# Moving the load ring of a two-attention decode kernel to the front of SBUF, in slots of 63744 bytes

## The chip, the core and the metric

The kernel runs on one core of one Trainium2 chip. The metric is the device time of one execution in microseconds (us). Three runs of the kernel before took 1010.08, 1009.97 and 1012.16 us; the median is 1010.08 us. Beside them stands one profiled execution, in which every instruction and every DMA packet was recorded. Its span, from the first to the last instruction, is 1008.4 us.

## The reference

One token `x` (448 numbers) goes through two attention blocks with a cache of 8192 positions, and a gate mixes the results:

```python
def block(x, k_cache, v_cache, wq, wo):       # A: 16 K/V heads; B: 8, each used by two q heads
    q = (x @ wq).reshape(16, 256)
    scores = einsum("hd,hkd->hk", q, k_cache) * 256 ** -0.5     # 8192 positions
    p = softmax(scores)
    o = einsum("hk,hkd->hd", p, v_cache)
    return o.reshape(16 * 256) @ wo
g = sigmoid((x * gate_w).sum())
out = g * A(x) + (1 - g) * B(x)
```

All is float32. Every number of the caches is used once (B's K and V for two heads at a time), so 432.02 MB have to come in from HBM and 1.8 KB go out.

## The kernel before

**The stream.** The host lays all inputs out as one stream, `in_stream_dram`, in the order in which the kernel uses them. `plan()` (lines 47 to 88) cuts it into 54 *fills*. A fill is what one buffer of the ring holds: 128 rows (one for each partition) of up to 15872 float32, that is 63488 bytes a partition and 8.13 MB in all. Fills 0 to 50 are one DMA each; fill 0 carries eight numbers more a row (`XG`). The last three fills are cut into 12 smaller DMAs, so that little is left to compute when the last bytes land. Within a fill stand pieces: tiles of K (`k`), of V (`v`), and the weights `wq` and `wo` of one of eight sets of heads (`NS`).

**The ring.** Line 464 takes a buffer from the pool `ring`, which has three (`SLOTS = 3`, line 34). Line 468 issues the DMA on SyncE's queue (SP). SP waits there until every instruction that used the slot's last content has ended; no other queue moves bulk data. The text calls the three buffers the first, second and third slot; fill n is in the slot n mod 3.

**The work on a fill.** Line 471 hands each piece to its function. `project` (line 211) makes q on TensorE from `wq`. `scores` (line 244) does the K tiles of two of a set's three units on TensorE (L255), then minimum (DVE, L261), exponential (ACT, L264) and a 32x32 transpose (DVE, L267). `scores_by_row` (line 271) does the third unit's K tiles on VectorE: a product in place in the slot (L277) and a sum (L281). `attend` (line 299) multiplies V by the weights of the softmax on TensorE (L307). `combine`, `column`, `project_o` and `emit_set` fold a head into the output, in small instructions. At the end L397 adds the last heads, L482 copies the result out of PSUM and L483 stores it.

**Order.** The schedule is manual (line 111): each engine runs its instructions in the order of the text, and the loop over `LOADS` (line 463) fixes it.

**Where the tiles lie.** Pools take their place in SBUF in the order in which they are opened, and tiles are padded to 32 bytes. In front lie 4224 bytes that the program keeps (4096 of them are `dynamic_dma_scratch_size`). Then come `const` (line 104) with 4736 bytes of masks, zeros, `xz`, `qb` and the like; `ring` (line 105); and `small` (line 106), with all other scratch tiles (`px`, `pr`, `qa`, `ob` and so on). A slot is 15880 float32, 63520 bytes. So the slots begin at bytes 8960, 72480 and 136000 of each partition, which are 0, 32 and 64 past a multiple of 256, and the third ends at 199520, which is 2912 bytes past 196608 (192 x 1024).

Of the kernel before, what the change touches and what calls it, by code (L numbers as in the profile page):

```python
# [7 lines left out]
F32 = mybir.dt.float32  # L8
# [6 lines left out]
P = 128  # L15
# [12 lines left out]
FULL = 15872  # L28
# [5 lines left out]
SLOTS = 3  # L34
# [6 lines left out]


XG = 2 * (KF + 1)
ATOM = {"xg": XG, "k": 2 * DH, "v": 2 * DH, "wq": 2 * DH, "wo": D}


def plan():

    size = {"xg": XG, "k": ROWS * DH, "v": ROWS * DH, "wq": WQ, "wo": 8 * D}
    per = len(UNITS) * NT  # L50
# [15 lines left out]
    for kind, i in items[:items.index(last[0])]:  # L66
        at, left = 0, size[kind]
        while left:
            step = min(left, room) // ATOM[kind] * ATOM[kind]
            if step:  # L70
# [24 lines left out]
def kernel(  # L95
# [5 lines left out]
    nc = tc.nc  # L101
    scale = DH ** -0.5

    const = ctx.enter_context(tc.tile_pool(name="const", bufs=1))
    ring = ctx.enter_context(tc.tile_pool(name="ring", bufs=SLOTS))
    small = ctx.enter_context(tc.tile_pool(name="small", bufs=2))
    ps_sc = ctx.enter_context(tc.tile_pool(name="ps_sc", bufs=2, space=PSUM))
    ps_o = ctx.enter_context(tc.tile_pool(name="ps_o", bufs=3, space=PSUM))
# [41 lines left out]
    nc.vector.tensor_scalar(rows4, rows4, 0.0, None, op0=OP.is_equal)  # L150
    any4 = const.tile([P, 1], F32, name="any4")
    nc.vector.tensor_reduce(any4, rows4, axis=AX.X, op=OP.add)
    ones = const.tile([P, 1], F32, name="ones")
    nc.vector.memset(ones, 1.0)

    in4 = const.tile([P, 2, NG], F32, name="in4")
# [258 lines left out]
    def piece(kind, i, at, view):  # L415
        n = view.shape[-1] // ATOM[kind]
        j0 = at // ATOM[kind]
        if kind == "xg":
            inputs(view[:, :KF + 1])
            GW[0] = view[:, KF + 1:]  # L420
        elif kind == "wq":
            project(i, j0, view.rearrange("p (c n) -> p c n", c=n))
            if j0 + n < 2 * KF + 1:
                pass
            elif i == 0:
                spread(0)
                prepare(GW[0])
            else:
                wait(1, spread, i)
        elif kind == "k":  # L430
            u, t = TILES[i]
            if u in BY_ROW:
                scores_by_row(u, t, 2 * j0, view.rearrange("p (j d) -> p j d", d=DH))
            else:
                scores(u, t, j0, view.rearrange("p (c n) -> p c n", c=n))
            if j0 + n < 2 * NG:
                return
            tick()
            if t == NT - 1:
                gather(u)  # L440
                wait(1, combine, u)
                wait(2, column, u)
        elif kind == "v":
            u, t = TILES[i]
            n = view.shape[-1] // DH
            attend(u, t, at // DH, n, view.rearrange("p (j d) -> p j d", d=DH))
            if at // DH + n == ROWS:
                if t == NT - 1:
                    take(u)
                    if u != TILES[-1][0]:  # L450
                        wait(1, project_o, u)
                if i >= len(TILES) - LEAD:
                    tick()
        elif kind == "wo" and i < NS - 1:
            emit_set(i, j0, view.rearrange("p (c n) -> p c n", c=n))
            if i == NS - 2 and j0 + n == 8:
                fold()
        else:
            for j in range(n):
                LAST[divmod(j0 + j, 2)] = view[:, j * D:(j + 1) * D]  # L460

    off = 0
    for fill in LOADS:
        buf = ring.tile([P, FULL + XG], F32, name="slot")
        c = 0
        for load in fill:
            n = sum(x[3] for x in load)
            nc.sync.dma_start(buf[:, c:c + n], stream[off:off + P * n].rearrange("(p n) -> p n", p=P))
            off += P * n
            for x in load:  # L470
                piece(*x[:3], buf[:, c:c + x[3]])
                c += x[3]
# [78 lines left out]
```

## Time and profile before

| What | Value |
|---|---|
| runs | 1009.97, 1010.08, 1012.16 us; median 1010.08 us |
| span of the profiled execution | 1008.4 us |
| the median less that span | 1.7 us |
| read from HBM | 432.02 MB |
| TensorE matmul busy | 584.2 us (58%) |
| VectorE (DVE) busy | 458.2 us (45%) |
| ScalarE (ACT) busy | 92.8 us (9%) |
| mean granted TensorE clock | 0.765 of full speed |

The span is the profiled execution's own time from its first to its last instruction; no other time of that execution was recorded, and what lies around it is taken to be the 1.7 us that separate it from the median of the runs. "Busy" is the time in which at least one instruction of an engine runs. The DMA rows count packets: one packet is what one of the core's 16 DMA engines moves in one go, here one partition's row of a load. A share over 100% means that packets on one engine overlap by a little.

### The profile page before, as it was taken

What the parts mean: (1) busy time and instruction counts of PE and PEld (TensorE: products, weight loads), DVE (VectorE), ACT (ScalarE), POOL (GpSimd) and SP (SyncE); (2) the same over time, 40 slices, a digit from 0 to 9 for tenths busy, and PEclk for the clock granted to TensorE, in tenths of its full rate; (3) what the DMA queues carried; (4) which work ended last, traced back from release to release, by engine and by line L of the source; (5) the groups of instructions that cost most, each with busy time, mean ns of one, the idle gap of its engine ahead of it and who ended that gap; (6) DMA issues with size and microseconds to landing.
All of it is one profiled execution on the core that took longest, in us unless ns stands there. A gap on an engine that the chain in (4) does not pass through costs nothing.

```text
span 1008.4 us, 7568 instructions
## 1 busy us (share of the span) xinstructions
PE 584.2 (58%) x3154; PEld 171.4 (17%) x3154; DVE 458.2 (45%) x644; ACT 92.8 (9%) x307; POOL 1.9 (0%) x10
## 2 busy tenths in 40 slices
PE   0855845664655555746646576655665637536567
PEld 0211211121111111212111121111211112111112
DVE  1386213961248521576214841248521585206851
ACT  0100100010100110001100000100110100101010
POOL 0000000000000000000000000000000000000000
PEclk9877787777787787877777767776787867877878
DMA  9999999999999999999999999999999999999997
GB/s 403 442 438 418 434 436 439 418 441 431 441 436 426 424 441 438 429 426 442 431 428 441 431 429 434 436 434 431 432 431 441 439 423 424 439 443 431 418 426 310
DMA packets 9113, 432.49 MB, mean 429 GB/s; under 512 B 1016, under 2 KB 1144, under 8 KB 1784
## 3 DMA queue, kind: packets, MB, share of 16 engines
q1 hardware_dynamic: 9080, 432.02, 99.2%
q8 instruction: 24, 0.39, 0.2%
q14 instruction: 9, 0.07, 0.0%
HBM read 432.02 MB, written 0.00 MB: 428 GB/s over the span
## 4 chain that ended last, share of the span: by engine, by line
DMA 72%; DVE 15%; PE 11%; ACT 1%; issue 1%; another core or an unknown queue 0%; SPq 0%; ACTq 0%; DVEq 0%
DMA slot<-in_stream_dram 72%; DVE sr L281 6%; DVE slot L277 6%; PE o L307 5%; PE sc L255 4%; PE sm L220 1%; ACT px L264 0%; DVE mn L261 0%; DVE pr L294 0%; ACT pxr L290 0%; DVE pr L267 0%; ACT ew L346 0%; DVE wr L353 0%; PE sm L371 0%; DVE mt L287 0%
## 5 line engine op out<-in xcount | busy, mean ns | idle before, releaser
L307 PE MATMUL o<-slot,pr 128*32 128x512 f32 (+1 forms) x1536 | 352.4, 764 | 220.2 <-DMA slot<-in_stream_dram 220.2
L255 PE MATMUL sc<-slot,qb 128*32 128x512 f32 x1024 | 199.0, 725 | 102.5 <-DMA slot<-in_stream_dram 102.3
L261 DVE TENSOR_REDUCE mn<-sc 128x1 f32<-128x512 f32 x64 | 44.1, 690 | 334.3 <-PE sc L255 311.5
L277 DVE TENSOR_TENSOR slot<-slot,qa 128x4096 f32<-128x4096 f32 (+7 forms) x40 | 142.6, 3565 | 43.6 <-DMA slot<-in_stream_dram 43.6
L307 PEld LDWEIGHTS o<-slot,pr 128*32 128x32 f32 (+1 forms) x1536 | 80.6, 143 | 403.5 <-DMA slot<-in_stream_dram 249.0
L281 DVE TENSOR_REDUCE sr<-slot 128x16 f32<-128x4096 f32 (+7 forms) x40 | 142.7, 3567 | 1.4
L255 PEld LDWEIGHTS sc<-slot,qb 128*32 128x32 f32 x1024 | 47.1, 132 | 221.2 <-issue 125.5
L264 ACT ACTIVATE px<-sc,st 128x512 f32<-128x512 f32 x64 | 44.0, 687 | 408.1 <-DVE st L262 366.5
L267 DVE STREAM_TRANSPOSE pr<-px 128x512 f32<-128x512 f32 x64 | 45.6, 713 | 59.5 <-ACT px L264 59.5
L220 PE MATMUL sm<-slot,xz 128*32 128x512 f32 x128 | 47.2, 717 | 36.8 <-DVE xz L193 22.9
L290 ACT ACTIVATE pxr<-sr,st 128x16 f32<-128x16 f32 x32 | 9.8, 308 | 372.9 <-DVE st L288 372.9
L371 PE MATMUL sm<-sel,ob 128*128 128x1 f32 (+1 forms) x96 | 18.2, 294 | 36.6 <-DVE ob L317 36.6
L317 DVE SCALAR_TENSOR_TENSOR ob<-o,half,ob 128x256 f32<-128x256 f32 x24 | 11.3, 473 | 43.6 <-ACT ob L316 43.6
L371 PEld LDWEIGHTS sm<-sel,ob 128*128 128x128 f32 x96 | 16.2, 237 | 60.5 <-DVE ob L317 54.9
L220 PEld LDWEIGHTS sm<-slot,xz 128*32 128x32 f32 x128 | 11.3, 129 | 67.0 <-issue 28.4
L294 DVE TENSOR_TENSOR pr<-pxr,cols 128x256 f32<-128x256 f32 x32 | 13.6, 426 | 15.9 <-ACT pxr L290 15.9
L237 PE MATMUL sm<-px,spread 64*128 64x256 f32 x16 | 7.1, 533 | 14.4 <-DVE es L347 14.4
L360 PE MATMUL sm<-ones,wr 1*128 1x1 f32 x48 | 9.6, 268 | 9.2 <-DVE wr L353 9.2
L316 ACT ACTIVATE ob<-o,half 128x256 f32<-128x256 f32 x24 | 11.3, 469 | 39.7 <-PE o L307 39.6
L380 PE MATMUL Y<-slot,ocs 128*1 128x448 f32 x112 | 14.1, 621 | 0.0
L360 PEld LDWEIGHTS sm<-ones,wr 1*128 1x128 f32 x48 | 7.8, 203 | 32.6 <-issue 32.6
L264 ACT ACTIVATION_READ_ACCUMULATOR px<-sc,st 128x1 f32 x64 | 12.3, 193 | 0.0
(73 smaller groups left out, 137.5 us busy)
## 6 DMA issues: line engine op xcount, KB each, us to landing
slot<-in_stream_dram SPq DMA_DIRECT2D x50, 7936.0 KB, 42.5
slot<-in_stream_dram SPq DMA_DIRECT2D x1, 7940.0 KB, 21.8
slot<-in_stream_dram SPq DMA_DIRECT2D x1, 4864.0 KB, 41.2
slot<-in_stream_dram SPq DMA_DIRECT2D x2, 2048.0 KB, 25.3
slot<-in_stream_dram SPq DMA_DIRECT2D x1, 3072.0 KB, 30.1
slot<-in_stream_dram SPq DMA_DIRECT2D x1, 1280.0 KB, 20.8
slot<-in_stream_dram SPq DMA_DIRECT2D x1, 1024.0 KB, 23.5
slot<-in_stream_dram SPq DMA_DIRECT2D x2, 512.0 KB, 24.8
```

The source lines that it names most:

```text
L220: nc.tensor.matmul(q[BLK * a:BLK * (a + 1), :], xz[:, c if c < KF else KF + a, :], w[:, j, :], start=(c == 0), stop=(c == KF), skip_group_ ...
L255: nc.tensor.matmul(sc[32 * g:32 * (g + 1), :], qb[:, e, at:at + 32], kt[:, j, :], start=(e == 0), stop=(e == 1), skip_group_check=True)
L261: nc.vector.tensor_reduce(mn, sc, axis=AX.X, op=OP.min)
L264: nc.scalar.activation(px, sc, AF.Exp, bias=st[:, 0, t:t + 1], scale=-1.0, accum_out=st[:, 1, t:t + 1])
L267: nc.vector.transpose(pr.rearrange("p (q r k) -> p q k r", r=BLK, k=2), px.rearrange("p (q k c) -> p q k c", c=BLK, k=2))
L277: nc.vector.tensor_tensor(kt, kt, QA[u][:, None, :].to_broadcast([P, n, DH]), op=OP.mult)
L281: nc.vector.tensor_reduce(sc[:, j0:j0 + n], kt, axis=AX.X, op=OP.add)
L294: nc.vector.tensor_tensor(pr, px[:, :, None, :].to_broadcast([P, ROWS // 2, NG * NT, 2]), cols[:, t].rearrange("p g r -> p (g r)")[:, None ...
L307: nc.tensor.matmul(O[u][w * g:w * (g + 1), :], pr[:, j // 2, :w], vt[:, j - j0:j - j0 + 2, :], start=(t == 0 and j < 2 * P // w), stop=(t ...
L360: nc.tensor.matmul(cl, WR.pop(u).rearrange("p c x m k -> p (c x m k)"), ones[:1, :], start=True, stop=True)
L371: nc.tensor.matmul(oc[:, e, :M], OB[u][:, e::2], SEL[u][:, :M], start=True, stop=True)
L380: nc.tensor.matmul(YY[0][32 * h:32 * h + 1, :], OC[s, r][:, e, m:m + 1], wt[:, j, :], start=False, stop=(s == NS - 2 and e == 1), skip_gro ...
```

## The change

The pool `ring` is opened ahead of `const`, and its tiles grow from 15880 to 15936 float32 (63744 bytes, 249 x 256). One tile goes ahead of the ring: `ones`, which was 1 column wide in `const`, becomes a view of a tile of 32 columns (128 bytes) in a pool of its own, `front`, so that the ring begins at 4224 + 128 = 4352 = 17 x 256. The slots then begin at 4352, 68096 and 131840, each a multiple of 256, and the third ends at 195584. `const` and `small` follow behind: `const` from 195584, `small` some 768 bytes higher than it was. What is loaded, the 54 fills, the DMAs, the order and the instructions stay as they are; `memset` of `ones` still stands at its place.

```diff
+SLOT = 15936
...
+    front = ctx.enter_context(tc.tile_pool(name="front", bufs=1))
+    ones = front.tile([P, 32], F32, name="ones")[:, :1]
+    ring = ctx.enter_context(tc.tile_pool(name="ring", bufs=SLOTS))
     const = ctx.enter_context(tc.tile_pool(name="const", bufs=1))
-    ring = ctx.enter_context(tc.tile_pool(name="ring", bufs=SLOTS))
     small = ctx.enter_context(tc.tile_pool(name="small", bufs=2))
...
-    ones = const.tile([P, 1], F32, name="ones")
     nc.vector.memset(ones, 1.0)
...
-        buf = ring.tile([P, FULL + XG], F32, name="slot")
+        buf = ring.tile([P, SLOT], F32, name="slot")
```

## The prediction

> **What bounds the kernel now.** I read the page from the top: the span, the 40 slices, the queues, the chain that ended last, the DMA issues. The slices ask first whether any engine is full.
>
> ```profile
> span 1008.4 us, 7568 instructions
> PE 584.2 (58%) x3154; PEld 171.4 (17%) x3154; DVE 458.2 (45%) x644; ACT 92.8 (9%) x307; POOL 1.9 (0%) x10
> ...
> DMA  9999999999999999999999999999999999999997
> ...
> q1 hardware_dynamic: 9080, 432.02, 99.2%
> ...
> DMA 72%; DVE 15%; PE 11%; ACT 1%; issue 1%; another core or an unknown queue 0%; SPq 0%; ACTq 0%; DVEq 0%
> ...
> slot<-in_stream_dram SPq DMA_DIRECT2D x50, 7936.0 KB, 42.5
> ```
>
> The DMA engines are the full ones: nine tenths or more in every slice but the last, and the packets of SP's queue alone fill 99.2% of the 16 engines' span, while TensorE has 58% and VectorE 45%. The chain says DMA for only 72%, because it walks back through whatever released a slot; the 28% of compute in it could be late only if a load were issued too late, so that the engines ran dry. Whether they do is told by the issues. The waits of SP's queue, and the load that came soonest after its issue of those I looked through (asked for by the window around its issue), read:
>
> ```profile
> SPq L468 <- DVE sr L281: 477.3, 24, 24.2
> SPq L468 <- PE o L307: 158.7, 15, 17.5
> ...
> slot<-in_stream_dram SPq DMA_DIRECT2D x1, 7936.0 KB, 34.7
> ```
>
> SP waits long for slots, but that is not lost time. A full load occupies the engines for 18.72 us (rows below), and the usual one lands 42.5 us after its issue, so it stands some 24 us behind others; the tightest, 34.7 us, still stood 16 us in the queue. The engines run on while SP waits. So time is made by the packets themselves: their number, their length, and the pauses between them.
>
> Now the packets slot by slot. The DMA view over a window of exactly 18.72 us that holds the 128 packets of one full fill (8.13 MB) and 16 completions gives the share of 16 engines' time that they took. Two windows in the first slot (171.20:189.92 and 565.17:583.89) and two in the second (302.24:320.96 and 808.91:827.63) all answer with the first row here. Fill 14, the fifth in the third slot (264.80:283.52), answers with the second, and three later fills in the third slot (320.96:339.68, 546.41:565.13 and 885.04:903.76) all with the third:
>
> ```profile
> q1 hardware_dynamic: 144, 8.13, 100.2%
> q1 hardware_dynamic: 144, 8.13, 100.3%
> q1 hardware_dynamic: 144, 8.13, 100.4%
> ```
>
> The same bytes in the same packets take 0.2 points longer in the third slot. 100.2% of 16 x 18.72 us over 128 packets is 2345 ns a packet; 100.4% is 2349 or 2350 ns. The first slot begins on a multiple of 256, the second 32 bytes past one, the third 64 past one and alone crosses byte 196608. First and second answer alike, so being 32 bytes off costs nothing that can be seen.
>
> **The change part by part.** No instruction, DMA, packet or wait is added or removed; every one gets other addresses.
>
> *Third slot.* This term makes the forecast. The extra of a packet costs a fill 0.2% of 18.72 us = 0.037 us; the shares are rounded to a tenth, so it lies between 0.1 and 0.3 points, 0.019 to 0.056 us. Seventeen full fills go to the third slot (fills 2, 5 and so on to 50). The clean windows show the extra from fill 17 on (320.96 us), and I carry it to all twelve from there; they show half of it on fill 14. The four before them had no undisturbed window, and I count them as nothing, with a full extra as the upper end. That is 12.5 x 0.037 = 0.46 us, between 12 x 0.019 = 0.23 and 17 x 0.056 = 0.95 us. Both things that set this slot apart, its 64 bytes and its end past 196608, go with the change, so it does not matter for the sum which it was. The queue is never dry, so what a packet saves is saved at the end.
>
> *First and second slot.* The first stays on a multiple of 256 and moves from 8960 to 4352: its own row, 100.2%, is the nearest; 0. The second loses its 32 bytes: by the equal rows 0, within 0.1 point either way (rounding), so at most 17 x 0.019 = 0.32 us up or down.
>
> *The slots' size.* 56 more bytes a row are never loaded; the packets keep 63488 bytes. 0. The last three fills' small loads begin at multiples of 256 within their slot, as they did: 0.
>
> *Masks and scratch.* `const` moves from below the ring to 195584 and above, `small` some 768 bytes up. Scratch already lies wholly past 199520, so the rows of before show what engines do up there:
>
> ```profile
> L261 DVE TENSOR_REDUCE mn<-sc 128x1 f32<-128x512 f32 x64 | 44.1, 690 | 334.3 <-PE sc L255 311.5
> ...
> L264 ACT ACTIVATE px<-sc,st 128x512 f32<-128x512 f32 x64 | 44.0, 687 | 408.1 <-DVE st L262 366.5
> L267 DVE STREAM_TRANSPOSE pr<-px 128x512 f32<-128x512 f32 x64 | 45.6, 713 | 59.5 <-ACT px L264 59.5
> ...
> L294 DVE TENSOR_TENSOR pr<-pxr,cols 128x256 f32<-128x256 f32 x32 | 13.6, 426 | 15.9 <-ACT pxr L290 15.9
> ```
>
> A transpose that reads and writes 128x512 above the edge takes 713 ns; a reduction of as many elements out of PSUM takes 690 ns. So an operand up there costs at most about 3% (23 ns in 713), and the equal time of ACT's 687 ns gives no reason for a gain larger than that. For `cols` at L294 that is 3% of 13.6 us, 0.4 us up or down in the whole run; the weight loads from `qb` stand beside the loads like it. All of it lies under the 16 us of the queue; without that cover each of the eight sets of heads would end 0.05 us later. Value 0. In the tail, after the last landing, only `ys` (L482) and the output's source lie in moved tiles:
>
> ```profile
> 985.78 18.75 DMA slot<-in_stream_dram
> 1004.53 0.04 issue
> 1004.57 0.99 PE Y L397 x32
> 1005.56 0.02 issue
> 1005.59 0.27 DVE ys L482
> ```
>
> That is 0.27 us on the path, between 0 and 0.01 us by the same 23 in 713. 0.
>
> **Sum.** The profiled execution goes from 1008.4 to 1007.9 us; its distance of 1.7 us to the median of the three runs stays, and 1010.08 - 0.46 gives **1009.6 us**.
>
> **The rivals.**
>
> *Nothing changes: 1010.1 us.* That would be if the third slot's extra did not come from its address but from its turn, or from how far the 16 engines have drifted apart. For it: fill 14 has only half of the extra, and an address is the same from the first fill on. Against it: from fill 17 on it returns in the windows of every third fill, while the neighbours stay at 100.2%. A sentence apart from these numbers: the Trainium skill, "SBUF — State Buffer", section "SBUF size: 192, 224, or 256?", gives 224 KiB as the active size of a partition on trn2 and 192 KiB for trn1 alone; by it byte 196608 is no edge on this chip, staying below it buys nothing, and the time would be this rival's. The trace has one slot that differs in two ways, so it cannot say.
>
> *Much faster: 1006.9 us.* Not only the steady extra but the long packets and pauses, which no clean window shows, might come from slots that lie off 256 and across the edge. The stretch from fill 3 to fill 49 prices them; the second row is a disturbed window in the second slot (133.62:152.34):
>
> ```profile
> DMA packets 6805, 382.42 MB, mean 433 GB/s; under 512 B 759, under 2 KB 759, under 8 KB 759
> ...
> q1 hardware_dynamic: 144, 8.13, 100.7%
> ```
>
> The stretch is 882.9 us long (58.56:941.49) and moved 382.42 MB. At the 8.13 MB in 18.72 us of a clean window (434.1 GB/s; the packets' exact sizes give 8.126 MB) that takes 881.0 us. The difference with rounding is 1.9 us, and 2.9 us if the 0.41 MB of other queues (382.42 less the 382.01 of SP's) is left out; over all 54 fills some 3.2 us. All of it would have to go. Against it: the disturbed window, at 100.7%, lies in the second slot, whose undisturbed ones read 100.2%, so address alone does not disturb; and to gain 0.2% (2.0 us) each of the 54 x 8 packets of an engine would have to become 4.7 ns shorter, below the 2345 ns of a slot that already lies on 256.
>
> *Slower: 1013.9 us.* Three slots with one phase modulo 256 can collide: TensorE or VectorE reads one slot while a DMA writes another at the same phase, and a write that meets a read waits. Before, the phases were 0, 32 and 64, so that nothing of the kind could show, or only now and then. The place is every packet of every fill; the nearest price is the one extra that the trace has, 4.7 ns (0.2 points), and two such waits a packet would be 54 x 8 x 2 x 4.7 ns = 4.1 us, less 0.3 for what the third slot no longer pays. From 4.7 ns a packet on, 2.0 us, it decides; one wait a packet is just that far. For it: engines are at work beside the loads all the time (the 58% and 45% above). Against it: the first slot lies on 256 already and reads 100.2%, whatever slot the engines read beside it. Apart from the numbers: the Trainium skill, "SBUF — State Buffer", section "SBUF: two separate sides", holds that DMA and engine ports are disjoint and that a DMA cannot be slowed by a compute instruction; by it this rival is worth nothing and the time is the forecast's. No row of before has three slots in one phase, so the trace leaves it a small chance.
>
> That the change does not do what it says would need another order of tiles than that in which pools are opened; the layout leaves 1024 bytes below 196608, and a slot past it would leave the time where it is, as in the first rival.
>
> **How the numbers follow.** Forecast, the extra goes: 0.60. Nothing changes: 0.15. Much faster: 0.15. Slower: 0.10. Forecast and first rival lie 0.5 us apart and both within 0.2% (2.0 us) of 1010.08, which is about what a measurement of this kernel can tell from no change: runs of before alone reach from 1009.97 to 1012.16. So within 0.2% gets 0.75, faster 0.15, slower 0.10. The terms alone reach from 1010.08 - 0.95 - 0.32 = 1008.8 to 1010.08 + 0.32 - 0.23 = 1010.2 us. As these two cases hold only 0.75, the range goes on toward the faster rival, past its half, to 1007.4, and up to 1011.8, where a collision of half the price would end (1010.08 + 2.05 - 0.3).
>
> **What will show it.** In the profile after, the windows of every third fill should read 100.2% like their neighbours from fill 17 on; where they still read 100.4%, the first rival holds. The mean over the long stretch should rise by 0.05%, which the rounded 433 GB/s may hide. If all windows read 100.4% or more, the phases collide, and the forecast is wrong in its slots of value 0. If they read under 100.2%, a slot on 256 was not at its best before. L294 and L482 should keep 426 and 274 ns within 3%, and SP's shortest queue should stay above 10 us; if it ran dry, the cover that I count on would be gone.

## The result, and the profile after

The kernel after takes 1008.94 us (median of 21 runs, 1008.36 to 1009.77) against 1010.32 us for the kernel before (median of 21 runs). The ratio is 0.9986, with a 95% interval from 0.998 to 0.9991: faster by 1.4 us, 0.9 to 2.0 us. That lies in the range of the prediction, within its 0.2% and on the side that it forecast, but it is three times the 0.46 us that it worked out.

The page of the kernel after, the lines that answer to those of before (line numbers are two higher from the loop on):

```profile
span 1007.3 us, 7568 instructions
PE 570.1 (57%) x3154; PEld 167.1 (17%) x3154; DVE 458.2 (45%) x644; ACT 92.9 (9%) x307; POOL 1.9 (0%) x10
...
DMA  9999999999999999999999999999999999999997
...
q1 hardware_dynamic: 9080, 432.02, 99.2%
...
DMA 72%; DVE 15%; PE 11%; ACT 1%; issue 1%; another core or an unknown queue 0%; SPq 0%; ACTq 0%; DVEq 0%
...
slot<-in_stream_dram SPq DMA_DIRECT2D x50, 7936.0 KB, 42.4
```

The bound is the same: as many packets and bytes, the same share, the same chain, only in 1.1 us less. The DMA view over 18.72 us with one undisturbed full fill answers alike in the three residues of the fill number modulo 3 (windows 508.38:527.10, 414.58:433.30 and 377.12:395.84), where before had 100.2, 100.2 and 100.4%:

```profile
q1 hardware_dynamic: 144, 8.13, 100.1%
```

All three have come down, not one. The view rounds to a tenth of a point, 2.3 ns a packet, so from here on I also use the packet records of the trace themselves: the mean duration of the 63488-byte packets from fill 17 on, without the few disturbed ones over 2380 ns. Before: 2343.05, 2343.02 and 2347.44 ns for the fills n mod 3 = 0, 1, 2. After: 2342.02, 2342.00 and 2342.01 ns, nearly every packet at exactly 2342.

The operations on moved masks and scratch (the groups view of the kernel after) stayed at 713, 426 and, within 1 ns, 274 ns; SP's queue had as long a lead (its waits, and the load issued soonest before its landing of those I looked through):

```profile
L269 DVE STREAM_TRANSPOSE pr<-px 128x512 f32<-128x512 f32 x64 | 45.6, 713 | 59.6 <-ACT px L266 59.6
L296 DVE TENSOR_TENSOR pr<-pxr,cols 128x256 f32<-128x256 f32 x32 | 13.6, 426 | 15.9 <-ACT pxr L292 15.9
...
L484 DVE COPY ys<-Y 128x112 f32<-128x112 f32 x1 | 0.3, 275 | 3.2 <-PE Y L399 3.2
```

```profile
SPq L470 <- DVE sr L283: 477.8, 24, 25.6
...
SPq L470 <- PE o L309: 156.8, 15, 17.3
```

```profile
slot<-in_stream_dram SPq DMA_DIRECT2D x1, 7936.0 KB, 34.6
```

The end of the chain that ended last:

```profile
963.69 20.73 DMA slot<-in_stream_dram
984.42 0.02 issue
984.43 18.49 DMA slot<-in_stream_dram
1002.92 0.04 issue
1002.96 1.47 PE Y L399 x32
1004.44 0.02 issue
1004.46 0.28 DVE ys L484
```

The last bytes land at 1002.92 us, against 1004.53 before. TensorE's last 32 products took 1.47 us here and 0.99 before, so 0.5 of these 1.6 us went again in this one execution; in the profiles of the three other kernels below with all slots aligned (`e1_aligned_crossing`, `e4_last`, `e7_source64`) they take 0.99 us. The span of the profiled execution is indeed on the high side: the 21 runs of the kernel after have spans from 1006.5 to 1007.5 us with a median of 1007.0.

### The profile page after: what moved, and what is told of

Its sections match the earlier page's. It is cut to its first block, busy times and chain, and to the rows that moved or that the text cites. A ratio compares the mean times of both kernels' runs of the same rounds, so it can differ in the third digit from the quotient of the medians.

```text
span 1007.3 us, 7568 instructions
## 1 busy us (share of the span) xinstructions
PE 570.1 (57%) x3154; PEld 167.1 (17%) x3154; DVE 458.2 (45%) x644; ACT 92.9 (9%) x307; POOL 1.9 (0%) x10
## 4 chain that ended last, share of the span: by engine, by line
DMA 72%; DVE 15%; PE 11%; ACT 1%; issue 1%; another core or an unknown queue 0%; SPq 0%; ACTq 0%; DVEq 0%
DMA slot<-in_stream_dram 72%; DVE sr L283 6%; DVE slot L279 6%; PE o L309 5%; PE sc L257 4%; PE sm L222 1%; ACT px L266 0%; DVE mn L263 0%; DVE pr L296 0%; ACT pxr L292 0%; DVE pr L269 0%; ACT ew L348 0%; DVE wr L355 0%; PE sm L373 0%
## 5 line engine op out<-in xcount | busy, mean ns | idle before, releaser
L309 PE MATMUL o<-slot,pr 128*32 128x512 f32 (+1 forms) x1536 | 342.3, 740 | 224.0 <-DMA slot<-in_stream_dram 223.9
L257 PE MATMUL sc<-slot,qb 128*32 128x512 f32 x1024 | 195.2, 713 | 112.1 <-DMA slot<-in_stream_dram 111.9
```

The costliest lines, as they stand in the source:

```text
L257: nc.tensor.matmul(sc[32 * g:32 * (g + 1), :], qb[:, e, at:at + 32], kt[:, j, :], start=(e == 0), stop=(e == 1), skip_group_check=True)
L309: nc.tensor.matmul(O[u][w * g:w * (g + 1), :], pr[:, j // 2, :w], vt[:, j - j0:j - j0 + 2, :], start=(t == 0 and j < 2 * P // w), stop=(t ...
```

## The experiments

The first four runs set two theories against each other: the **phase theory** (the extra comes from slots that begin off a multiple of 256 bytes) and the **edge theory** (it comes from rows that cross byte 196608). Each time is a median of 11 runs, set against 33 runs of the kernel before on the same chip: 1010.26 us beside `e1` to `e4`, 1010.47 beside `e5` to `e8`, 1010.33 beside `e9` to `e12`.

### Alignment without the move, and the move without alignment

Alignment alone (`e1_aligned_crossing`): the pools in before's order, and only the slot's length changed.

```diff
-        buf = ring.tile([P, FULL + XG], F32, name="slot")
+        buf = ring.tile([P, 15936], F32, name="slot")
```

> Slots on multiples of 256 as in the kernel after (8960, 72704, 136448), but behind the masks as before, so that the third ends at 200192 and still crosses byte 196608. Phase theory (the extra comes from starting off a multiple of 256): every clean window reads 100.1%, as in the kernel after, and the time is some 1.4 us under before, about 1008.9. Edge theory (it comes from crossing 196608): the third slot's windows keep 100.4%, the others 100.2% or 100.1%, and the time stays within 0.5 us of before, about 1010.1. If both matter, the third slot lies between, at 100.2 to 100.3%.

Measured: 1008.70 us, ratio 0.9985 (0.9976 to 0.9994). Packets 2342.02, 2342.00 and 2342.02 ns; the windows 508.15:526.87, 414.33:433.05 and 376.87:395.59 all answer

```profile
q1 hardware_dynamic: 144, 8.13, 100.1%
```

The move alone (`e2_below_phases`), against the kernel after:

```diff
-SLOT = 15936
+SLOT = FULL + XG
```

> The order of the kernel after, ring in front, third slot ending at 194912, but the slots are again 63520 bytes apart and begin 0, 32 and 64 past a multiple of 256 (4352, 67872, 131392), as before. Phase theory: the third slot's windows read 100.4% as before, the time stays within 0.5 us of before, about 1010.1. Edge theory: every window reads 100.1%, the time is some 1.4 us under before, about 1008.9.

Measured: 1010.40 us, ratio 0.9998 (0.999 to 1.0007). The windows 508.75:527.47, 414.73:433.45 and 377.15:395.87:

```profile
q1 hardware_dynamic: 144, 8.13, 100.2%
q1 hardware_dynamic: 144, 8.13, 100.2%
q1 hardware_dynamic: 144, 8.13, 100.4%
```

No row crosses 196608 any more, and the pattern of before stands as it was (2343.06, 2342.97 and 2347.43 ns). The edge theory falls in both runs: one whole half of the change, the pools' order, does nothing, and the 56 bytes of padding do all of it.

### The ring at the very end

`e4_last` opens `small` ahead of the ring, so that 26 KB of one slot lie above 196608:

```diff
+    small = ctx.enter_context(tc.tile_pool(name="small", bufs=2))
+    front = ctx.enter_context(tc.tile_pool(name="front", bufs=1))
+    ones = front.tile([P, 56], F32, name="ones")[:, :1]
     ring = ctx.enter_context(tc.tile_pool(name="ring", bufs=SLOTS))
-    small = ctx.enter_context(tc.tile_pool(name="small", bufs=2))
...
-    ones = const.tile([P, 1], F32, name="ones")
...
-        buf = ring.tile([P, FULL + XG], F32, name="slot")
+        buf = ring.tile([P, 15936], F32, name="slot")
```

> All slots on multiples of 256, but the ring stands last: 32000, 95744 and 159488, so that 26 KB of the third slot's rows lie above 196608, where before it was 2.9 KB; all masks and scratch lie below. Phase theory: as the kernel after, 100.1% everywhere, about 1008.9. Edge theory with a fixed price for crossing: third slot 100.4%, about 1010.1. Edge theory with a price for each byte above: nine times the extra, some 40 ns a packet, third slot above 101.5%, and some 4 us over before, about 1014.

Measured: 1008.62 us, ratio 0.9983 (0.9974 to 0.9992); 2342.01, 2342.00 and 2342.02 ns, and 100.1% in the windows 508.25:526.97, 414.47:433.19 and 377.03:395.75. Bytes above 196608 cost nothing either. The Trainium skill, "SBUF — State Buffer", section "SBUF size: 192, 224, or 256?", gives 224 KiB a partition on trn2, so that 192 KiB is no edge. These three runs agree with it: with aligned slots, rows across byte 196608 take the 2342.0 ns of rows below it, and with off slots wholly below it the extra stays.

### All three slots off by the same

`e3_below_all64` puts every slot 64 past a multiple of 256, against the kernel after:

```diff
-    ones = front.tile([P, 32], F32, name="ones")[:, :1]
+    ones = front.tile([P, 48], F32, name="ones")[:, :1]
```

> The kernel after with 64 more bytes in front: all three slots begin 64 past a multiple of 256 (4416, 68160, 131904), none reaches 196608. Phase theory: all three slots carry the extra of before's third, 100.4% in every window, three times its cost: some 1.0 to 1.5 us over before, about 1011.5. Edge theory: as the kernel after, 100.1% everywhere and about 1008.9.

Measured: 1011.11 us, ratio 1.001 (1.0001 to 1.0019). 2346.65, 2346.67 and 2346.67 ns; the windows 509.17:527.89, 414.95:433.67 and 377.35:396.07 all read

```profile
q1 hardware_dynamic: 144, 8.13, 100.3%
```

So 64 past costs 4.65 ns a packet when all slots are there. The phase theory had put 100.4% and 1.0 to 1.5 us over before; it is 100.3% and 0.85 us, the right direction and a smaller size. Now the puzzle: in before one slot was 32 past and one 64 past, but only one residue of fills had a large extra. Here I looked up the addresses in the DMA instructions of the built program and found that the text ahead of the prediction is wrong on one point. The pool hands out its buffers in another order than that of their addresses: fill 0 goes to byte 8960 (0 past), fill 1 to 136000 (64 past, the one that crosses), fill 2 to 72480 (32 past), and so on in turn. What I had called the third slot, with its 100.4%, was the one at 32 past that crosses nothing; and the crossing one at 64 past had read 100.2%. The same holds for "third slot" in the expectations above: the windows meant are those of fills 2, 5, 8 and so on. Three runs ask what the offset does:

`e5_all32` (front tile of 40 columns instead of 32), `e6_all128` (64 columns) and `e12_all16`, which writes 16 bytes into each slot:

```diff
-        c = 0
+        c = 4
         for load in fill:
```

> The kernel after with 32 bytes more in front: all three slots begin 32 past a multiple of 256. Any-offset theory (a start off a multiple of 256 costs each packet some 4.7 ns, whatever the offset): as with all three slots at 64, 2347 ns a packet, every window 100.3 to 100.4%, about 1011. Offset-of-64 theory (32 is free, and what before's first and second slot showed over 100.13% was third-slot packets in their windows): 100.1% everywhere, about 1008.9. My prediction's value for the second slot was 0.

> All three slots 128 past a multiple of 256. Any-offset theory: 100.3 to 100.4% in every window, about 1011. A theory in which the price grows with the bytes between the boundary below and the start: some 9 ns a packet, 100.5%, about 1013. A theory in which 128 is a full boundary: 100.1%, about 1008.9.

> The kernel after, with each row written 16 bytes further into its slot, so that all three begin 16 past a multiple of 256. Any-offset theory: 100.3 to 100.5% in every window, 4.7 to 5.6 ns a packet, about 1011.3. If a start that is not even a multiple of 32 costs one more step on the way, more than that, 100.5% and more, over 1012.

Measured: 32 past, 1011.54 us, ratio 1.001 (1.0001 to 1.0018), 2347.60 to 2347.65 ns. 128 past, 1011.05 us, ratio 1.0005 (0.9996 to 1.0014), 2346.28 to 2346.35 ns. 16 past, 1012.07 us, ratio 1.0015 (1.0006 to 1.0024), 2348.59 to 2348.65 ns. One window of each, 509.37:528.09 in the first, 508.95:527.67 in the second, 509.56:528.28 in the third:

```profile
q1 hardware_dynamic: 144, 8.13, 100.4%
```

```profile
q1 hardware_dynamic: 144, 8.13, 100.3%
```

```profile
q1 hardware_dynamic: 144, 8.13, 100.4%
```

Over the 2342.0 ns of an aligned packet: 6.6 ns at 16 past, 5.6 at 32, 4.65 at 64, 4.3 at 128. Each of the four offsets costs, the smallest the most; 128 is no boundary that helps. The any-offset theory holds in that every offset pays, and its 4.7 ns is the right size; that the price is the same whatever the offset does not hold, and that it grows with the offset still less: it falls. At 16 past neither expectation came whole: the share is that of the any-offset theory, the 6.6 ns and 1012.07 us are over its numbers, and of what was put for a start off 32 the time came (over 1012) and the share (100.5% and more) did not.

The price goes by packets far more than by bytes. In the tail the loads are smaller; their packets of 38912 bytes take 1439.0 ns in the kernel after and 1442.7 with all slots at 64 past, those of 4096 bytes 159.0 and 162.0. So 63488 bytes pay 4.65 ns, 38912 bytes 3.7 and 4096 bytes still 3.0.

### The read side

`e7_source64` puts 16 zeros ahead of the stream in HBM, so that every read moves by 64 bytes and the writes stay; `e8_both64` moves reads and writes (front tile of 48 columns). The sums are not touched.

```diff
-    off = 0
+    off = 16
     for fill in LOADS:
...
-        "stream": _np.concatenate([
+        "stream": _np.concatenate([_np.zeros(16, _np.float32)] + [
```

> The kernel after with 16 zeros ahead of the stream in HBM: every row is read from 64 past a multiple of 256, and written to slots that begin on one. Destination theory (only the written address matters): as the kernel after, 100.1%, about 1008.9. Source-too theory or relative theory (what costs is an offset of the read, or that read and write lie differently to a multiple of 256): 100.3 to 100.4% or more, about 1011.

> Rows are read from 64 past and written to 64 past a multiple of 256. Destination theory: as with all slots at 64 alone, 100.3 to 100.4%, about 1011. Relative theory: read and write lie alike, so nothing is paid, 100.1%, about 1008.9. Source-too theory: both extras, some 9 ns a packet, 100.5% and more, about 1013.

Measured: reads moved alone, 1008.75 us, ratio 0.9984 (0.9975 to 0.9993), 2342.00 to 2342.02 ns. Both moved, 1011.05 us, ratio 1.0006 (0.9997 to 1.0015), 2346.65 ns. A window of each, 508.31:527.03 and 509.08:527.80:

```profile
q1 hardware_dynamic: 144, 8.13, 100.1%
```

```profile
q1 hardware_dynamic: 144, 8.13, 100.3%
```

In these runs only the written address matters, and not how it lies to the read one. The Trainium skill, "DMA: Bandwidth & Descriptors", section "How a descriptor splits into AXI transactions", says that a transfer whose start is off a multiple of 256 bytes has to begin at the boundary below and pays beats (steps of 32 bytes) for bytes that it does not need, and it says so of reads. The trace shows the multiple of 256, but on the write side; moving the reads by 64 bytes changed nothing that the packets show (where the stream itself begins in HBM, no run shows). If that held for writes too, 64 past would by the beats of the Trainium skill pay one more than 32 past, which is an estimate; measured, it pays 1 ns less.

### One off slot, and two in another order

Single prices of 4.65 (64 past) and 5.6 ns (32 past) make 10.25 ns for before's three residues; measured over 2342.0 are 1.05 + 1.02 + 5.43 = 7.5. The **additive theory** (each off packet pays for itself) can't say where 2.75 ns went, nor why the fills at 64 past showed only 1.0 of their 4.65 ns. The rival is a **backlog theory**: an aligned packet's write takes less than its packet lasts, because something else, the read for one, sets the pace; what an off packet loses is then made up by aligned ones, until it is too much. Three slots in pools of their own, used in the order of their addresses, against the kernel after:

```diff
-    ring = ctx.enter_context(tc.tile_pool(name="ring", bufs=SLOTS))
+    rings = [ctx.enter_context(tc.tile_pool(name=f"ring{k}", bufs=1)) for k in range(SLOTS)]
...
-    for fill in LOADS:
-        buf = ring.tile([P, SLOT], F32, name="slot")
+    for k, fill in enumerate(LOADS):
+        buf = rings[k % SLOTS].tile([P, SLOT + (16, 48, 0)[k % SLOTS]], F32, name="slot")
```

That is `e9_lone64`, with fills at 0, 64, 0; `(0, 8, 0)` gives 0, 0, 32 (`e11_lone32`), and `(8, 8, 0)` gives 0, 32, 64 (`e10_order_32_64`).

> The kernel after, with the three slots as pools of their own, used in the order of their addresses, so that fills 1, 4, 7 and so on go to a slot 64 past a multiple of 256 and all others to slots on one. Additive theory (every packet to an off slot pays for itself): those fills carry 4.7 ns a packet, 100.3%, the others 100.1%, time 0.6 to 0.8 us over the kernel after, about 1009.4. Backlog theory (an aligned packet's write takes less time than its read and so makes up for what an off packet's write lost just before): one off fill among three costs little, under 1.5 ns a packet in any of them, time within 0.3 us of the kernel after, about 1008.9.

> Only the third fill of each three goes to an off slot, 32 past a multiple of 256. Additive theory: these fills at 100.4%, 5.6 ns a packet, time 0.8 to 0.9 us over the kernel after, about 1009.6. Backlog theory: under 2 ns a packet in any fill, time within 0.3 us of the kernel after, about 1008.9.

> As before in its offsets, but in another order of use: fill 0 on a multiple of 256, fill 1 at 32, fill 2 at 64 past one (before: 0, then 64, then 32). Additive theory with prices by offset: the fills at 32 carry the large extra wherever they stand, here the windows of fills 1, 4, 7. Backlog theory: the second off fill in a row carries it whatever its offset, here the fills at 64 (fills 2, 5, 8), at 100.3 to 100.4%, and the fills at 32 stay near 100.2%. Time about that of before, 1010.3, by both.

Measured, with the packets by residue:

| Offsets of fills 0, 1, 2 | packets, ns | time, us | ratio to before (95%) |
|---|---|---|---|
| 0, 64, 0 (`e9_lone64`) | 2342.02, 2342.12, 2342.12 | 1008.99 | 0.9989 (0.998 to 0.9997) |
| 0, 0, 32 (`e11_lone32`) | 2342.17, 2342.00, 2342.14 | 1009.25 | 0.999 (0.9981 to 0.9999) |
| 0, 32, 64 (`e10_order_32_64`) | 2342.84, 2343.76, 2346.81 | 1010.53 | 0.9999 (0.9991 to 1.0008) |

The windows 508.22:526.94, 414.43:433.15 and 376.96:395.68 of `e9_lone64` all answer with the row below; the middle one holds fill 22, at 64 past:

```profile
q1 hardware_dynamic: 144, 8.13, 100.1%
```

Those of `e10_order_32_64`, 508.73:527.45, 414.65:433.37 and 377.12:395.84, are at 0, 32 and 64 past:

```profile
q1 hardware_dynamic: 144, 8.13, 100.2%
q1 hardware_dynamic: 144, 8.13, 100.2%
q1 hardware_dynamic: 144, 8.13, 100.4%
```

One off fill among three costs 0.2 to 0.3 ns where the additive theory needs 4.65 and 5.6; and with the order turned round the large extra moved from the fills at 32 past to those at 64, the second off fill in a row in both cases. The additive theory falls, and the backlog theory's packets came. Of its times, that of `e9_lone64` came; that of `e11_lone32` is 0.31 us over the kernel after, a hair past the 0.3 put for it, and undisturbed packets make only 0.05 of that.

The packet records of before show the backlog itself. Each of the 16 engines moves eight packets of a fill; I took the packets in the order in which they start, in groups of 16, from fill 17 on. In the fills at 64 past, the first off ones, the first four groups take 2342.0 ns as if they were aligned, and the next four 2342.2, 2343.3, 2345.0 and 2345.65. In the fills at 32 past, written next, all eight take 2346.4 to 2348.1, near the 2347.6 of a kernel with all slots at 32. In the aligned fills behind them the first four take 2346.05, 2344.7, 2343.0 and 2342.2, and the last four 2342.0 to 2342.1. The cost appears some packets late and fades some packets late. In `e10_order_32_64` it does the same with the offsets turned round, and there the fills at 64 past, now second, take 2346.4 to 2347.1 in all eight groups.

The sums give a size: two off fills lose 10.25 ns and 7.5 (before) or 7.4 (`e10_order_32_64`) come out, so an aligned packet makes up for about 2.8 ns, if all eight of a fill do so alike; two of them for up to 5.6, which is why one lone fill is nearly free. Where in the chip the backlog stands no run shows; that the read sets the pace is an argument, not a measurement.

## Why the prediction was right or wrong

**What bounds the kernel: right.** The packets of SP's queue are the time. In every run the median moved as the sum of its packets did, to within 0.5 us.

**The extra in one residue of fills goes: right in kind and about right in size, for the wrong slot.** 0.46 us was the term; the trace's records (what undisturbed packets take over 2342 ns, summed over the run and divided by 16 engines) give 0.605 us before and 0.028 after, so 0.58 us. But I took the slot for the one that crosses 196608 and lies 64 past, from an order of buffers that I had assumed and not looked up. That the term came all the same is luck: the change puts all three slots on 256, so it did not matter which of them carried the extra.

**First and second residue, value 0: the step that failed.** The prediction put it that "being 32 bytes off costs nothing that can be seen", because two residues read 100.2% alike. The row that it read was not even that of the slot at 32, but that of the one at 64. And equal rows prove a value of 0 only if one of them is free of the extra, and none was: the aligned fills' 100.2% held 1.05 ns a packet of what off fills had left behind, and the fills at 64 past had handed most of theirs on. Each residue gave 0.11 us (0.131 to 0.017 and 0.152 to 0.044). The bound that I set for it, 0.32 us in one residue, held. The 2345 ns that the prediction read from 100.2% were too many as well: the records have 2343.0, since the share is rounded and holds the 16 completions of the window too.

**The small loads of the tail, value 0: wrong.** The prediction gave as reason that they begin at multiples of 256 within their slot, but the slots did not. An off packet pays whatever its size, and the ten loads of the last two fills all went to off slots. The packets of the last three fills sum to 41.48 us an engine before and 41.22 after, 0.25 us.

These terms make 0.58 + 0.11 + 0.11 + 0.25 = 1.05 us, and all packets of SP's queue together took 1.10 us less an engine (1000.31 and 999.21). The span fell by 1.1, the median by 1.4 (0.9 to 2.0). That the terms meet the span so closely is partly chance: the stretch from the start of the first packet that carries rows to the end of the last is 1.5 us shorter, 1.1 in packets and 0.4 in pauses, and TensorE's last products took 0.5 back. Whether the pauses belong to the change isn't settled: they are 2.7 to 3.2 us in the profiles of the four kernels with all slots aligned, and 3.0 to 3.4 in those of the eight with two or three slots off.

**Masks and scratch, value 0: right** (the rows above), and the queue never ran dry.

**The rivals.** "Nothing changes" weighed the third slot's turn against its address; the truth has something of both, since it is the address that costs and the turn that decides where the cost shows. "Much faster" wanted the disturbed windows to go; they stayed: the packets over 2380 ns of the full fills from 1 on cost 1.13 us an engine before and 1.10 after. "Slower" fell with the first row of the kernel after: three slots in one phase read 100.1%; where all lie in one phase off 256 (`e3_below_all64`, `e5_all32`, `e6_all128`, `e12_all16`) it is the offset that costs, and that half was in no rival. That it is not the shared phase shows in `e10_order_32_64`, where the fills at 64 past pay 4.8 ns with every slot in a phase of its own. (In this rival's price the third slot saves 0.3 us, against 0.46 in the sum; by the sum it would have been 1013.7 us.)

**The test of a slot on 256.** The text said that windows under 100.2% would mean that "a slot on 256 was not at its best before". That is what came.

No run beats the kernel after beyond its interval: alignment alone (1008.70), the ring at the end (1008.62) and the moved reads (1008.75) stand at 0.9983 to 0.9985 of before, it at 0.9986.

## What to carry to other kernels

Where the DMA engines are full, let each row that is written in SBUF begin on a multiple of 256 bytes: pad the buffer's length to one, as the 56 bytes here, and see that the first of them begins on one. The price was 3 to 5 ns a packet from 4096 to 63488 bytes at 64 past, so it is 0.2% with rows of 62 KB and grows as the rows shrink, to 1.9% at 4096 bytes. And a cost in the records of a full pipe stands where the slack runs out, not where it arises: a quiet neighbour isn't proof that its own setting is free, so change one setting for all buffers at once before calling it so.

## What the runs showed of the hardware that was not expected

Off packets of 63488 bytes cost 6.6, 5.6, 4.65 and 4.3 ns at 16, 32, 64 and 128 bytes past a multiple of 256; why the smaller offset costs more is open. An aligned packet gives back about 2.8 ns, by the sums above. The extra also takes time to set in: with all slots at 64 past the packets' means are 2343.8 to 2345.3 ns in the first eight fills and 2346.3 to 2347.1 from fill 12 on, which neither theory gives. The first eight fills are uneven in the kernel after too, where their means are 2342.3 to 2345.2 ns; the reason stays open. From there on an aligned stream is remarkably even: of the 6400 packets of the kernel after, 6143 took exactly 2342 ns, and 221 of the other 257 are in those first eight fills.
